# A hand-ordered schedule rewritten: attention fused with a gated feed-forward layer on one Trainium2 core

## The chip, the core and the metric

The kernel runs on one core of one Trainium2 chip. The core has four engines that compute: TensorE (PE in the profile; PEld is its weight load), VectorE (DVE), ScalarE (ACT) and GpSimd (POOL). SyncE (SP) only issues transfers. Each engine works off its own list of instructions strictly in order, so an instruction that waits holds up everything behind it on that engine. Transfers run on 16 DMA engines that all queues share. The metric is the time of one execution in microseconds. The kernel before takes 406.1 us, the median of three runs (405.54 to 406.79).

## The reference

The input is q, k and v, each 8 batches x 12 heads x 448 positions x 64 channels in fp32, a scalar tau of 0.1, and two weight matrices. The output is 3584 x 768 in fp32.

```python
q_n = q / (norm(q, axis=-1, keepdims=True) + 1e-06)
k_n = k / (norm(k, axis=-1, keepdims=True) + 1e-06)
attn = softmax(q_n @ k_n.transpose(0, 1, 3, 2) / tau)
x = (attn @ v).transpose(0, 2, 1, 3).reshape(8 * 448, 768)
h = x @ w_in                      # 768 -> 2048
out = (h * clip(h + 3, 0, 6) / 6) @ w_out   # 2048 -> 768
```

## The kernel before, in words

**Pairs.** Two heads are worked on together as a pair: 6 pairs to a batch, 48 in all, numbered through. Pairs 0 to 5 are the first batch, 6 to 11 the second. The two heads lie in the two halves of 128 partitions.

**Two regimes.** Pairs 18 to 47 run in a loop. Everything for pairs 0 to 17, about the first 120 us, is written out by hand in the list `PLAN`: strings of short operations that are issued in exactly that order. No scheduler moves anything (`tc.manual_schedule()`); the compiler only adds the waits that the data need. Each operation lands at the end of the list of its own engine, so the order in `PLAN` matters only within an engine. `ORDER` says which kind of product a unit `U` is.

**Operations.** A letter a, v or p picks ScalarE, VectorE or GpSimd. Items j are q or k of two pairs at once: items 0 and 1 are the queries and keys of pairs 0 and 1, items 2 and 3 those of pairs 2 and 3, and so on.

- `LQ.j`, `LV.d`: SyncE issues the load of item j (one transfer of 448 KB) or of the values of two pairs (four of 128 KB). Seven buffers hold the items: `LQ.j` waits for `NM.(j-7)`. Only eight of SyncE's transfers can be open at a time, because each waits for the eighth before it.
- `SQ.j` squares an item (for items 0 and 1 in pieces: `SQ.1.a.7.4` is four of the fourteen columns of 64). `RE.j` (DVE) adds the squares up; `NO.d` turns the sums of items 2d and 2d+1 into reciprocal norms: four small ScalarE instructions (ln, exp, ln, exp; lines 255 to 262), or with `v` two on ScalarE and then an add and a reciprocal on VectorE. `NM.j` multiplies the item by them into bf16.
- `TR.j`: seven TensorE transposes of an item into a PSUM bank (`Y`, `Z`, or the next of a ring). `CK`, `CQ`, `CS` copy keys and queries of one pair out of it to SBUF. From item 14 on the transposes are transfers (`XD`).
- `SC.i.g`, `EX.i.g`, `VA.i.g`: scores of pair i, group g of 4 (TensorE), exponential (ScalarE), product with the values (TensorE). `VC.i` casts the values to bf16 for it. `FI.i` (DVE) divides by the sum; `BK.i` and `CX.i` transpose the output on TensorE and copy it to `xT`, or `XP`/`XB` do it by transfer.
- Scores of pairs 0 to 5 go to two double-width PSUM tiles `SC`, so one exponential covers 128x896; `OPEN` then gives that PSUM to a ring of six banks, and from pair 6 on an exponential covers 128x448.
- `W`: the next of eight weight transfers, issued by GpSimd (line 910). The first four are `w_in`, the first two of them its left half; the last four are `w_out`.
- `U`: one unit of the feed-forward layer. The first 30 are `mm1_unit`: six matmuls of 128x448 with `w_in` (line 567). `UA` is its relu on ScalarE (line 576), `UV` the gated product on VectorE (line 582). The first unit needs `CX.0` to `CX.5` and both of the first two `W`. The last six are products with `w_out` (line 614) and need all eight `W`.
- `DP.n`: n matmuls on zeros, 128x248 (line 922), and `D.n`: 128x512 (line 917). Nothing reads what they write.
- `WS` and `GL` make sums of weights and copies for the loop (DVE).

The weights are taken like this, and a unit of the left half asks for two of them:

```python
    def next_weights():
        o, w = weights.pop(0)
        nc.gpsimd.dma_start(out=o, in_=w)
...
    def mm1_unit(b, fc):
        needs(*(("CX", i) for i in range(b * HP, (b + 1) * HP)))
        assert len(weights) <= 6 - 2 * (2 * fc // FCN)
```

Of the kernel before, what the change touches and what calls it, by code (L numbers as in the profile page):

```python
# [1097 lines left out]
```

## Time and profile before

| what | us |
|---|---|
| three runs, median (lowest to highest) | 406.1 (405.54 to 406.79) |
| the profiled execution, whole | 404.91 |
| its span, first to last instruction | 403.1 |
| PE, DVE, ACT, POOL busy | 395.5, 286.4, 278.3, 234.0 |

The profile shows one execution. Its span of 403.1 us and 1.8 us around it make its own 404.91 us, which is 1.2 us under the median of the runs. Busy times of matmuls overlap, since they are pipelined, and their ends are modelled: a busy TensorE is read from how closely the starts follow each other. A row of the timeline gives start and length in us, engine, line, operation, output<-input with their shapes and how many were merged; in square brackets stands the idle time before it and what ended it. Lines are those of the kernel before.

### The profile page before, as it was taken

What the parts mean: (1) busy time and instruction counts of PE and PEld (TensorE: products, weight loads), DVE (VectorE), ACT (ScalarE), POOL (GpSimd) and SP (SyncE); (2) the same over time, 40 slices, a digit from 0 to 9 for tenths busy, and PEclk for the clock granted to TensorE, in tenths of its full rate; (3) what the DMA queues carried; (4) which work ended last, traced back from release to release, by engine and by line L of the source; (5) the groups of instructions that cost most, each with busy time, mean ns of one, the idle gap of its engine ahead of it and who ended that gap; (6) DMA issues with size and microseconds to landing.
All of it is one profiled execution on the core that took longest, in us unless ns stands there. A gap on an engine that the chain in (4) does not pass through costs nothing.

```text
span 403.1 us, 9619 instructions
## 1 busy us (share of the span) xinstructions
PE 395.5 (98%) x3696; PEld 234.3 (58%) x3696; DVE 286.4 (71%) x503; ACT 278.3 (69%) x609; POOL 234.0 (58%) x228
## 2 busy tenths in 40 slices
PE   7999999999999999999999999999999999999996
PEld 4666656555655556556555556555565556555563
DVE  5898768766998777776867888687656566644663
ACT  5999998798467686786858768668658755225230
POOL 7799655662384997488386865766665500510070
PEclk9999999999999999999999999999999999999999
DMA  8999989979988659786989659976963523130134
GB/s 289 281 254 257 216 247 230 156 125 230 187 213 220 139 128 228 171 222 130 180 216 212 152 130 164 182 192 145 192 154 76 112 46 67 41 79 21 26 73 99
DMA packets 91566, 65.32 MB, mean 162 GB/s; under 512 B 56064, under 2 KB 89984, under 8 KB 91520
## 3 DMA queue, kind: packets, MB, share of 16 engines
q1 hardware_dynamic: 87408, 58.02, 62.8%
q0 software_dynamic: 3712, 6.29, 9.0%
q8 instruction: 29, 0.48, 0.5%
q10 hardware_dynamic: 400, 0.39, 0.3%
q14 instruction: 17, 0.14, 0.1%
HBM read 47.19 MB, written 11.01 MB: 144 GB/s over the span
## 4 chain that ended last, share of the span: by engine, by line
PE 94%; DVE 3%; DMA 1%; ACT 0%; issue 0%; DVEq 0%; ACTq 0%
PE M L567 24%; PE M L740 17%; PE PV L462 13%; PE Y L567 6%; PE M L422 6%; PE Z L567 5%; PE Y L740 4%; PE Z L740 4%; PE M L614 3%; PE M L820 2%; PE Z L422 2%; PE PV L922 2%; PE Z L820 1%; PE Y L422 1%; DVE n L238 1%; PE SC L422 1%
## 5 line engine op out<-in xcount | busy, mean ns | idle before, releaser
L440 ACT ACTIVATE at<-M 128x448 bf16<-128x448 f32 x200 | 99.9, 568 | 16.4 <-PE M L422 14.4
L567 PE MATMUL M<-xT,w_in_sb 128*128 128x448 bf16 x522 | 110.8, 352 | 0.0
L567 PEld LDWEIGHTS <-w_in_sb 128*128 128x128 bf16 x768 | 72.0, 98 | 62.6 <-issue 2.8
L274 POOL TENSOR_TENSOR nrm<-big,r 128x896 bf16<-128x896 f32 (+1 forms) x48 | 79.5, 1662 | 26.1 <-ACT r L262 19.3
L576 ACT ACTIVATE u<-M,bias 128x448 bf16<-128x448 f32 x87 | 57.0, 655 | 25.2 <-PE M L567 24.8
L582 DVE SCALAR_TENSOR_TENSOR gT<-u,M 128x448 bf16<-128x448 bf16 x76 | 46.7, 618 | 36.8 <-ACT u L576 36.3
L226 POOL TENSOR_TENSOR big<-big 128x896 f32<-128x896 f32 (+3 forms) x39 | 63.9, 1641 | 10.9 <-DMA big<-in_k_dram 5.7
L462 PEld LDWEIGHTS <-at 128*128 128x128 bf16 (+1 forms) x1536 | 54.9, 97 | 22.8 <-issue 13.5
L462 PE MATMUL PV<-vx,at 128*128 128x65 bf16 (+1 forms) x1536 | 64.3, 194 | 0.2 <-DVE on L483 0.2
L238 DVE TENSOR_REDUCE n<-big 128x14 f32<-128x896 f32 (+1 forms) x50 | 51.7, 1041 | 5.6 <-ACT big L224 4.6
L379 POOL COPY km<-tT 64x128 bf16<-64x128 bf16 x34 | 12.8, 376 | 58.1 <-DMA tT<-nrm 45.1
L769 POOL TENSOR_TENSOR big<-big 128x384 f32<-128x384 f32 x11 | 11.8, 1076 | 54.6 <-ACT big L788 54.5
L740 PEld LDWEIGHTS <-gT 128*128 128x128 bf16 x288 | 27.8, 98 | 20.0 <-DVE gT L718 0.6
L740 PE MATMUL M<-w_out_sb,gT 128*128 128x384 bf16 x208 | 37.9, 326 | 0.1
L440 ACT ACTIVATE at<-Z 128x448 bf16<-128x448 f32 x49 | 27.7, 565 | 9.9 <-PE M L422 7.3
L483 DVE TENSOR_TENSOR on<-PV,rc 128x512 bf16<-128x512 f32 x48 | 33.2, 691 | 1.7
L293 POOL CAST vx<-big 128x512 bf16<-128x512 f32 x44 | 33.2, 757 | 1.2 <-DMA big<-in_v_dram 1.1
L422 PE MATMUL M<-tT,kz 64*128 64x448 bf16 (+1 forms) x175 | 31.6, 351 | 0.0
L740 PEld LDWEIGHTS <-gs 128*128 128x128 bf16 x224 | 21.5, 98 | 14.8 <-DVE gs L718 0.4
L567 PE MATMUL Y<-xT,w_in_sb 128*128 128x448 bf16 x132 | 28.6, 352 | 0.0
L440 ACT ACTIVATE at<-Y 128x448 bf16<-128x448 f32 x45 | 25.7, 570 | 3.1 <-PE Z L422 1.7
L740 PE MATMUL M<-w_sum,gs 128*128 128x384 bf16 x144 | 26.3, 326 | 0.0
(130 smaller groups left out, 561.7 us busy)
## 6 DMA issues: line engine op xcount, KB each, us to landing
big<-in_v_dram SPq DMA_DIRECT2D x96, 128.0 KB, 4.4
big<-in_k_dram SPq DMA_DIRECT2D x24, 448.0 KB, 4.9
big<-in_q_dram SPq DMA_DIRECT2D x24, 448.0 KB, 4.4
out_dram<-o SPq DMA_DIRECT2D x107, 96.0 KB, 2.2
w_in_sb<-in_moe_w_in_dram POOLq DMA_DIRECT2D x4, 768.0 KB, 10.2
w_out_sb<-in_moe_w_out_dram POOLq DMA_DIRECT2D x4, 768.0 KB, 9.2
tT<-nrm SPq DMA_TRANSPOSE x34, 3.3
xT<-on SPq DMA_TRANSPOSE x25, 3.8
```

Of the source, the lines that this page charges most:

```text
L226: engines[e].tensor_tensor(out=o, in0=i, in1=i, op=ALU.mult)
L238: nc.vector.tensor_reduce(out=n2s[d % 2][:, j % 2, c], in_=sq[:, :, :, :].rearrange("p g c d -> p (g c) d")[:, c, :], axis=AX.X, op=ALU.add,)
L274: engines[e].tensor_tensor(out=nrm[:, :, g, :].rearrange("p c g d -> p g c d"), in0=raw_of[j][:, g, :, :], in1=rs[d % 2][3][:, j % 2, :] . ...
L293: (engines[e].copy if e == "a" else engines[e].tensor_copy)(out=o, in_=f)
L422: nc.tensor.matmul(o, ks, qt[rows], start=True, stop=True)
L440: nc.scalar.activation(out=o, in_=x, func=AF.Exp, scale=inv_tau)
L462: nc.tensor.matmul(pv_out(j, h), at[rows, n, q_cols(i // HP, j)], vt[rows, 3 + h if name == "M" else 5 * h + int(name[1]), :], start=(name ...
L483: nc.vector.tensor_tensor(out=on[:, :, :, :].rearrange("p j h d -> p h j d"), in0=pv4[:, :, :, 0:D], in1=rc[:, :, :].to_broadcast([128, 2, ...
L567: nc.tensor.matmul(ps[:, 0:S], w_in_sb[:, cc, fc * 128 : (fc + 1) * 128], x[:, cc, 0:S], start=(cc == 0), stop=(cc == CC - 1),)
L576: nc.scalar.activation(out=u[:, :], in_=ps[:, 0:S], func=AF.Relu, bias=half_bias, scale=1.0 / 6.0)
L582: nc.vector.scalar_tensor_tensor(out=g[:, fc, c0 : c0 + S], in0=u[:, :], scalar=1.0, in1=ps[:, 0:S], op0=ALU.min, op1=ALU.mult,)
L740: nc.tensor.matmul(m, lhs[:, c, :], rhs[:, c, c0 : c0 + width], start=(base is None and c == 0), stop=(c == KC - 1), skip_group_check=True,)
```

## The change

Only `PLAN` changes (the file has one line less, so every later line number is one lower). Both plans hold the same transfers and the same real TensorE work; the units `U`, and the parts of each pair, are issued in another order and some operations move to another engine. Of the dummies, 86 `DP` and 10 `D` become 69 `DP`: 58 of them ahead of the first scores and 11 behind, where before 37 `DP` and the 10 `D` stand ahead and 49 behind.

- `NO.0.0` and `NO.1` to `NO.6` take the form with two instructions on VectorE.
- To ScalarE: `SQ.4`, `SQ.11`, `SQ.21`, `CQ.10`, `CQ.12`. The pieces of items 0 and 1 are dealt out anew: GpSimd keeps one of item 0, VectorE has two of item 1, ScalarE the other four. From ScalarE to GpSimd: `SQ.6`, `SQ.13`, `SQ.15`, `SQ.18`, `SQ.20`. From ScalarE to VectorE: `CX.9`, `CK.12`.
- From VectorE to GpSimd: `NM.2`, `NM.18`, `VC.3`, `SQ.22`. From GpSimd to VectorE: `VC.4`, `VC.9`, `VC.15`, `VC.18`, `VC.19`.
- Products with the values come earlier: `VA.0.0` ahead of `SC.0.3`, `BK.0` ahead of `SC.2.0`. `CK.2` and `CK.3` stand behind `FI.0` and `CX.0`, `CK.6` and `CK.7` behind the copies of pair 2's output.
- On GpSimd the second `W` stands behind `SQ.6` to `SQ.9`, `NM.2` to `NM.7`, `VC.3` and `VC.5`; before, behind `SQ.4`, `SQ.7` to `SQ.9` and `NM.3` to `NM.6`. The third stands behind `SQ.10`, `SQ.13`, `SQ.12`. The fifth to eighth stand behind `SQ.17`, `VC.14`, `SQ.19` and `SQ.18`.
- On SyncE `LQ.7` goes ahead of `LV.1`, `LV.2` ahead of `LQ.9` to `LQ.11`, `LV.4` behind `LQ.13` and `LQ.12`.

Of the 35 and 34 lines the first half is shown; the rest follows the lists above.

```diff
--- before.py
+++ after.py
@@ PLAN @@
-    "LQ.1 DP.5 SQ.1.a.11.3 SQ.1.p.4.3 DP.1 SQ.1.a.0.4 LQ.0 SQ.0.p.8.6 DP.2 DP.4 LQ.3 LQ.2 SQ.1.v.7.4 RE.1.1",
-    "SQ.0.a.0.6 RE.1.0 NO.0.1 LQ.5 LQ.4 SQ.0.v.6.2 DP.6 NM.1.p.0 D.10 RE.0.1 DP.3 NM.1.p.1 RE.0.0 DP.8 NO.0.0",
-    "SQ.3.a.0.7 LV.0 DP.2 SQ.2.a.0.7 NM.0.p.0 RE.3 RE.2 NM.0.p.1 TR.1.Y DP.2 TR.0.Z CK.0.v DP.4 SQ.4.p.0.7 CQ.0.v",
-    "SQ.5.a.0.7 LQ.6 NO.1 LV.1 LQ.7 SC.0.0.0 SC.0.1.1 DP.5 DP.3 CQ.1.v EX.0.0 RE.5 RE.4 NM.3.p SC.0.2.0 CK.1.v DP.3",
-    "EX.0.1 DP.3 EX.0.2 NM.2.v DP.3 SC.0.3.1 TR.3.Y LQ.8 NO.2 EX.0.3 DP.3 SC.1.0.0 TR.2.Z EX.1.0 VC.0.v SC.1.1.1 DP.2",
-    "EX.1.1 VA.0.0 CK.2.v VC.1.v VC.3.v NM.4.p NM.5.p VA.0.1 LQ.9 SC.1.2.0 SQ.6.a.0.7 LQ.11 DP.5 DP.2 SC.1.3.1 EX.1.2",
-    "CQ.2.v LQ.10 LV.2 VA.0.2 VA.0.3 DP.3 SC.2.0.0 DP.2 EX.1.3 CK.3.v SC.2.1.1 EX.2.0 TR.4.Y SC.2.2.0 SQ.7.p.0.7",
-    "EX.2.1 RE.6 FI.0 RE.7 LV.3 VA.1.0 SQ.8.p.0.7 SC.2.3.1 CQ.3.v VC.2.v CQ.5.v VA.1.1 EX.2.2 SC.3.0.0 EX.2.3 VA.1.2",
-    "NO.3 RE.8 SC.3.1.1 CQ.4.v EX.3.0 DP.2 DP.4 EX.3.1 VA.1.3 TR.5.Z SC.3.2.0 W SQ.9.p.0.7 EX.3.2 FI.1 CK.4.v BK.0.Y",
-    "VA.2.0 SC.3.3.1 RE.9 LV.4 EX.3.3 NO.4 VA.2.1 VA.2.2 VA.2.3 SC.4.0.0 EX.4.0 NM.6.p DP.2 SC.4.1.1 SQ.10.p.0.7 W",
-    "SQ.11.p.0.7 EX.4.1 CX.0.v TR.6.Y CK.5.v FI.2 CQ.7.v VA.3.0 BK.2.Z RE.10 SC.4.2.0 EX.4.2 NM.7.p CQ.6.v VA.3.1",
-    "SC.4.3.1 DP.2 EX.4.3 CX.2.v SC.5.0.0 RE.11 VA.3.2 EX.5.0 SC.5.1.1 VA.3.3 VC.4.p SC.5.2.0 FI.3 VC.5.p EX.5.1",
-    "BK.1.Y TR.7.Z SC.5.3.1 CX.1.v CK.6.v CK.7.v VA.4.0 EX.5.2 DP.2 CS.7.v EX.5.3 BK.3.Y VA.4.1 LQ.12 CS.6.v OPEN",
-    "DP.2 CX.3.v NO.5 SC.6.0 VA.4.2 VA.4.3 SC.6.1 SC.6.2 EX.6.0 NM.8.p FI.4 EX.6.1 EX.6.2 SC.6.3 TR.8 BK.4 VA.5.0",
-    "CX.4.v VA.5.1 CQ.8.v SC.7.0 VA.5.2 EX.6.3 NM.9.p CQ.9.v VC.6.p VA.5.3 SC.7.1 FI.5 EX.7.0 SC.7.2 TR.9 SC.7.3",
-    "NM.10.p CK.8.v VA.6.0 EX.7.1 EX.7.2 VC.8.p CS.8.v W BK.5 SQ.12.p.0.7 LQ.13 VA.6.1 VA.6.2 SC.8.0 EX.7.3 CS.9.v",
-    "VA.6.3 CK.9.v DP.1 EX.8.0 CX.5.v SC.8.1 SC.8.2 VC.7.p FI.6 LQ.15 EX.8.1 U UA SQ.13.a.0.7 LV.5 U TR.10 EX.8.2 UA",
...
+    "DP.13 LQ.1 SQ.1.v.0.4 SQ.1.v.11.3 DP.9 DP.5 DP.3 SQ.1.a.7.4 LQ.0 SQ.0.p.8.6 SQ.1.a.4.3 SQ.0.a.0.6 DP.7 RE.1.0",
+    "RE.1.1 SQ.0.a.6.2 DP.5 LQ.2 LQ.3 NO.0.1 NM.1.p.0 NM.1.p.1 TR.1.Y RE.0.1 RE.0.0 NO.0.0.v LQ.5 DP.6 SQ.2.a.0.7",
+    "SQ.3.a.0.7 DP.4 RE.2 NM.0.p.0 RE.3 CK.1.v LQ.4 CK.0.v DP.3 NM.0.p.1 TR.0.Z SQ.4.a.0.7 LV.0 CQ.0.v DP.3 NO.1.v",
+    "SC.0.0.0 RE.4 NM.2.p LQ.6 SQ.5.a.0.7 SC.0.1.1 DP.4 VC.0.v DP.2 DP.2 EX.0.0 SC.0.2.0 EX.0.1 NM.3.p RE.5 VA.0.0",
+    "EX.0.2 SC.0.3.1 TR.2.Y CQ.1.v CQ.2.v CQ.3.v EX.0.3 SC.1.0.0 VA.0.1 LQ.7 VA.0.2 SC.1.1.1 VA.0.3 SQ.6.p.0.7 NO.2.v",
+    "SQ.7.p.0.7 EX.1.0 EX.1.1 SC.1.2.0 NM.4.p TR.3.Y VC.1.v LV.1 FI.0 CK.2.v EX.1.2 SC.1.3.1 BK.0.Z SC.2.0.0 VA.1.0",
+    "CX.0.v VC.2.v LQ.8 EX.1.3 LV.2 EX.2.0 CK.3.v SC.2.1.1 RE.6 VA.1.1 VA.1.2 SC.2.2.0 LQ.10 VA.1.3 EX.2.1 SC.2.3.1",
+    "TR.4.Y EX.2.2 FI.1 SC.3.0.0 EX.2.3 VA.2.0 NM.5.p VC.4.v SC.3.1.1 LQ.9 SQ.8.p.0.7 CQ.5.v EX.3.0 TR.5.Z EX.3.1",
+    "SC.3.2.0 VA.2.1 CQ.4.v VA.2.2 VC.3.p RE.7 CK.4.v DP.1 VA.2.3 BK.1.Y W FI.2 SC.3.3.1 EX.3.2 SC.4.0.0 NO.3.v",
+    "EX.3.3 SC.4.1.1 RE.8 SQ.9.p.0.7 CK.5.v VA.3.0 EX.4.0 EX.4.1 RE.9 SC.4.2.0 LQ.11 EX.4.2 VA.3.1 SC.4.3.1 VA.3.2",
+    "CX.1.v VA.3.3 EX.4.3 FI.3 NM.6.p NM.7.p BK.2.Z SC.5.0.0 SC.5.1.1 TR.6.Y NO.4.v LV.3 VA.4.0 EX.5.0 EX.5.1 VC.5.p",
+    "CQ.7.v CX.2.v SC.5.2.0 TR.7.Z EX.5.2 W VA.4.1 CQ.6.v VA.4.2 SQ.11.a.0.7 NM.8.p VC.7.p SC.5.3.1 CS.6.v VC.6.p",
+    "BK.3.Y CK.6.v CK.7.v EX.5.3 OPEN CS.7.v SC.6.0 VA.4.3 CX.3.v DP.2 EX.6.0 SC.6.1 EX.6.1 FI.4 SC.6.2 SC.6.3 NM.9.p",
+    "TR.8 EX.6.2 VA.5.0 SQ.10.p.0.7 BK.4 VA.5.1 VA.5.2 RE.11 EX.6.3 SC.7.0 EX.7.0 CX.4.v VA.5.3 CQ.9.v CQ.8.v SC.7.1",
+    "SC.7.2 TR.9 FI.5 EX.7.1 SC.7.3 LQ.13 CK.9.v VA.6.0 CS.8.v VA.6.1 EX.7.2 CK.8.v SQ.13.p.0.7 CS.9.v BK.5 VA.6.2",
+    "SC.8.0 VA.6.3 SC.8.1 EX.7.3 CX.5.v RE.10 FI.6 EX.8.0 SC.8.2 U RE.13 EX.8.1 U SC.8.3 EX.8.2 VA.7.0 SC.9.0 VA.7.1",
+    "NO.5.v LQ.12 SQ.12.p.0.7 VA.7.2 UA UV LV.4 U W VA.7.3 LQ.15 UA UV EX.8.3 EX.9.0 UA NM.11.p SC.9.1 RE.12 SC.9.2",
+    "UV U FI.7 NM.10.p TR.11 EX.9.1 NO.6.v LQ.14 VC.9.v EX.9.2 UA CS.10.v W TR.10 VC.8.p LV.5 SC.9.3 CK.10.v",
+    "SQ.15.p.0.7 CQ.11.a U VA.8.0 CQ.10.a VA.8.1 XP.6 EX.9.3 VA.8.2 CS.11.v LQ.17 NM.12.p UV CK.11.v VA.8.3 FI.8 UA",
...
```

## The prediction, made before the result was known

> **What bounds the kernel now.** I read the page's busy shares first, then its chain of waits, then busy time by stretch, then single engines' timelines about the joints between stretches.
>
> ```profile
> PE 395.5 (98%) x3696; PEld 234.3 (58%) x3696; DVE 286.4 (71%) x503; ACT 278.3 (69%) x609; POOL 234.0 (58%) x228
> PE 94%; DVE 3%; DMA 1%; ACT 0%; issue 0%; DVEq 0%; ACTq 0%
> ```
>
> TensorE holds 94% of the chain. Part of that is dummies, so I look at stretches (columns: span, then PE, PEld, DVE, ACT, POOL busy, granted clock, DMA share, GB/s). I cut at the first exponential (12.87), at the end of the last one of pair 5 (35.16), at the first unit U (42.85) and near the end of the plan (118).
>
> ```profile
> 12.87:35.16 22.29, 21.85 (x286) 14.25 (x285) 19.79 (x39) 21.22 (x39) 20.96 (x16) 1.00 1.06 267
> 35.16:42.85 7.69, 7.69 (x138) 5.21 (x134) 5.95 (x22) 7.53 (x21) 7.68 (x8) 1.00 1.11 247
> 42.85:118.00 75.15, 75.15 (x750) 43.88 (x749) 57.27 (x98) 60.52 (x135) 40.22 (x38) 1.00 0.98 200
> ```
>
> In the first row everything is full: ScalarE, TensorE with its 49 dummies, GpSimd, and the DMA engines. From 42.85 on TensorE never idles. Next, ScalarE in the first stretch:
>
> ```profile
> 12.87 2.54 ACT L440 ACTIVATE at<-SC 128x896 bf16<-128x896 f32 x3
> 15.28 0.24 ACT L255 ACTIVATE ln<-n 128x28 f32<-128x28 f32 x1
> ...
> 16.34 2.17 ACT L440 ACTIVATE at<-SC 128x448 bf16<-128x448 f32 x3
> 18.40 0.95 ACT L224 ACTIVATE big<-big 128x896 f32<-128x896 f32 x1
> ...
> 28.99 6.17 ACT L440 ACTIVATE at<-SC 128x896 bf16<-128x896 f32 x8
> ```
>
> Exponentials follow each other with only norms and one square between, so this row of work sets when pair 5 ends. Last, the joint at the first unit, and the weight transfer that it needs:
>
> ```profile
> 28.86 0.70 POOL L910 DMA_DIRECT2D w_in_sb<-in_moe_w_in_dram x1
> ```
> ```profile
> 42.54 0.35 PE L422 MATMUL M<-tT,kz 64*128 64x448 bf16 x2
> 42.85 0.35 PE L567 MATMUL M<-xT,w_in_sb 128*128 128x448 bf16 x1
> ```
> ```profile
> w_in_sb<-in_moe_w_in_dram POOLq DMA_DIRECT2D x1, 768.0 KB, 13.7
> ```
>
> The second W is issued at 28.86 and lands 13.7 us later (transfers issued in a window of its own), at 42.56: 0.3 us before the unit starts. TensorE came to it without idling, so today the weights are just in time. A plan that brings TensorE there earlier meets this transfer.
>
> The set of real TensorE operations ahead of the first U is the same in both plans, and so is the set behind it. With no idle time after 42.85, the end moves by what the first U moves, plus any new idle time behind it. I work on that.
>
> **The change part by part.** *ScalarE before the first exponential.* Gained: SQ.4, whose load, the sixth, is issued at 3.29 and lands 7.4 us later, at 10.70 (0.95 us, done 11.65). Lost: two of four norm instructions, half of the 1.06 us (15.28 to 16.34) that a norm takes. Then ln and exp of NO.1 to 12.15, SQ.5 to 13.0: first exponential at about 13.0, against 12.87. The first scores are ready by 12.5 (GpSimd's four half-size NM end near 11.0, transposes 0.55, copies 0.7).
>
> *ScalarE from there to the end of pair 5.* Kept: per pair three wide exponentials at 0.81 a step and one narrow at 0.45, six pairs: 17.3. Before, three norms at 1.06 and SQ.6 at 0.85 made 21.3, and waits and joints 1.0: the 22.29. After: three half norms at 0.5, SQ.11 in place of SQ.6, 0.85: 19.65. Walking the TensorE, VectorE and GpSimd lists beside it with row durations (reduce 1.0, copy 0.3, divide 0.85, GpSimd 896-wide 1.65, cast 0.57) I find waits of 0.2 for SC.3.0 and 0.2 at pair 5, so 20.0. Pair 5 ends at 33.0 instead of 35.16.
>
> *Norms on VectorE.* Seven times an add and a reciprocal on 28 columns. Not in the trace; nearest are the one-column memset, 0.06, and the 8-column reciprocal, 0.21: between 0.1 and 0.6 for the two, I take 0.35. It lies beside exponentials, but what is queued behind (RE.4, RE.8, CQ.7) moves by as much; that is in the walk.
>
> *Dummies.* 38 fewer behind the first scores, at 0.106 each (8.79, 1.54 for 13 with overlap): 4.0 us less on TensorE in a stretch where it was 21.85 of 22.29 busy. That is what lets TensorE follow the faster exponentials. Worth nothing by itself.
>
> *From the end of pair 5 to the first U.* Same work: 42.85 less 36.12, the first exponential of pair 6, is 6.73; before, a norm stood ahead of it (35.03 to 36.12) and now NO.5 is later. First exponential of pair 6 at 33.4, so TensorE is ready for the first U at 40.1: 2.7 us earlier.
>
> *The second W.* GpSimd can start NM.2 at 12.6 (NO.1 on VectorE). Up to the second W stand NM.2 to NM.7 and SQ.6 to SQ.9, ten at 1.65, two casts at 0.57 and the first W at 0.8: 18.4. Issue at 31.05, 2.2 us later than before; none of the ten waits for a load or norm in my walk. How long it takes is not settled by one row: the eight weight transfers took 7.3, 7.6, 9.8, 10.0, 10.4, 10.9, 13.7 and 14.4. The two longest were issued while another weight transfer was still open; the two shortest in quieter stretches. Here the loads of SyncE are the usual crowd (LQ.13, LQ.12, LV.4, LQ.15), but the first W, issued at 24.7, runs nearly alone because LQ.13 waits for NM.6 until 28.8. I take the median, 10.2: landing at 41.25, first U at 41.3. Ends: 7.3 (40.1, TensorE binds) and 13.7 (44.75).
>
> *SyncE.* LQ.7 now stands ahead of LV.1 and waits for NM.0 (11.0); LV.1 and LQ.8 queue behind. Four value transfers take 2.0 us (LV.1 lands from 14.6 to 16.2 before), so LV.1 lands near 17.5, for a first use at 19.1: free, and the DMA engines still have LQ.6 in hand until 14.2. LQ.13 waits for NM.6 (28.8) with LQ.12 and LV.4 behind it; these are used after 36, and the pause is what empties the queues for the first W.
>
> *Third and fourth W.* The third stands behind SQ.12, which waits for RE.10 (40.4): issue 42.1 instead of 40.00. The fourth stands behind NM.11 and NM.10: 46.3 instead of 42.89. The ninth U, at 60.3, is the first to need them. 46.3 and 10.2 is 56.5, free; with 14.4 it would cost 0.4.
>
> *Behind the first U.* TensorE has 19.0 us from the first to the ninth U; ScalarE in it 22 exponentials at 0.43, 8 relus at 0.62, three copies and two half norms: 16.9; VectorE 15. SC.10.0 to SC.10.2 follow copies CK.10, CK.11 and the fifth UV with under 0.1 us to spare, so I put 0.2 there; ends 0 and 1.0. Further on, XP.6 no longer holds SyncE's later loads as long (it waited to 51.28 for FI.7). The eighth W leaves at about 81 instead of 85.73, for a first use near 94.5 (95.89 before): covered, and if that cover went, a W of 14.4 us would cost 1. GpSimd gets five net squares and multiplies of 1.65 but sheds four casts; it idles 4 to 8 us at a time there.
>
> *Sum.* 41.3 less 42.85 is -1.55; plus 0.2: -1.35. The profiled 404.91 becomes 403.55. The runs' median lies 1.2 higher: 404.7.
>
> [...] The first 18 dummies take 3.90 us, 0.207 apart, the 13 at 8.79 run at 0.106: TensorE starts at half speed. [...]
>
> **The rivals.** (a) *W in time.* If the second W takes 7.3 to 9.8, the first U is at 40.1 to 40.9: 403.4 to 404.3. For: the first W runs alone. Against: five of eight rows are longer. (b) *W late, slower than before.* One mechanism: the second W takes as long as before or longer. At 13.7 the first U is at 44.8, 406.1 + 1.95 + 0.2 = 408.2; it decides against the change from 11.8 on (42.85). For: same neighbours on the DMA engines, full at 1.06 to 1.11. Against: it no longer queues behind an open W. [...] (d) *Scores don't get faster.* GpSimd's NM.6 and NM.7, or VectorE's copies, hold pair 5 until 35: TensorE meets W at about 42.85, 406.1. For: NM.7 ends at 30.5 in my walk and SC.5.3 follows at once. Against: it has 0.4 to spare.
>
> **How the numbers follow.** The likeliest, 0.40: W at 10 to 10.9, first U 41.1 to 42.0, 404.5 to 405.5; 404.7 is the point. By its own 0.3% line (1.2 us, about what a measurement of this kernel can tell from no change) it is 0.25 faster and 0.15 the same. (a) 0.18, faster. (d) with W between 11 and 12: 0.14, the same or slightly slower: 0.12 and 0.02. (b) 0.20, slower. (c) 0.08, slower. Faster 0.43, same 0.27, slower 0.30. The range leaves out (c) and the far end of (a): 403.4 to 408.2.
>
> **What would show it.** Right: the first exponential of pair 6 near 33.4; the second W issued near 31; TensorE idle about 1 us ahead of its first L567, ended by that transfer; that first L567 between 41 and 42; no idle TensorE after it. Wrong: no idle time there (W early, or scores late), granted clock under 1.00 after 40, or TensorE idle between the first and ninth unit, ended by VectorE's copies.

## The result and the profile after

The changed kernel takes **408.3 us** (median of 10 runs, 407.39 to 410.35) against 405.96 for the kernel before (10 runs, 405.13 to 407.14): ratio 1.0063, interval 1.0042 to 1.0084. It is slower by 0.6%, where I forecast 404.7 and a gain. (The ratios leave out single runs that lie more than 1.5% above a kernel's fastest; the medians and ranges in this text hold all runs.) The profiled execution took 408.33 us, span 406.5, mean granted clock 0.996; line numbers are one lower than before.

The page's busy shares and chain of the changed kernel:

```profile
PE 394.1 (97%) x3669; PEld 234.1 (58%) x3669; DVE 292.4 (72%) x518; ACT 274.1 (67%) x594; POOL 239.3 (59%) x228
PE 85%; DMA 6%; DVE 4%; ACT 1%; SPq 1%; issue 1%; POOL 1%; DVEq 0%; POOLq 0%; ACTq 0%
```

TensorE holds 85% of the chain instead of 94%: transfers have come into it (6% instead of 1%), VectorE a little (4% instead of 3%). Busy time by stretch, cut at the first exponential, at the end of the last one of pair 5, at the first unit and where the plan's last part ends (columns as in the prediction):

```profile
13.13:35.49 22.36, 19.12 (x262) 12.51 (x260) 20.10 (x47) 19.68 (x32) 21.04 (x16) 0.92 1.02 262
35.49:43.39 7.90, 7.05 (x116) 4.79 (x116) 6.92 (x19) 7.47 (x18) 5.93 (x6) 1.00 1.10 269
43.39:122.87 79.48, 77.72 (x756) 44.88 (x756) 62.03 (x106) 59.46 (x134) 51.30 (x43) 1.00 0.97 191
```

Pair 5 ends at 35.49, hardly elsewhere than before (35.16), although ScalarE was busy for only 19.68 of the 22.36 us: it waited. The granted clock is 0.92 in this row. And TensorE, which never idled behind the first unit before, does so for 1.76 us in the third row. What TensorE waited for between 13 and 122 us, by the view of waits (total, times, longest):

```profile
PE Z L495 <- DVE on L482: 1.4, 1, 1.4
PE M L566 <- DMA w_in_sb<-in_moe_w_in_dram: 0.8, 1, 0.8
PE SC L421 <- ACT at L439: 0.7, 2, 0.3
PE M L421 <- ACT at L439: 0.6, 1, 0.6
PE M L421 <- DVE gT L581: 0.6, 1, 0.6
PE Z L421 <- DVE kz L340: 0.5, 1, 0.5
PE M L421 <- POOL km L378: 0.4, 1, 0.4
PE Y L421 <- DVE o L626: 0.3, 1, 0.3
```

The span grew by 3.4 us. The first unit stands at 43.39 instead of 42.85: 0.55. The rest, 2.85, is lost behind it, at three places, where I compare the distance from one matrix product to the next with its usual one: 1.6 us at 53.2 to 55.1 (0.60, 0.94 and 0.26 over the usual, less the 0.19 that one such step always has), 0.5 at 105 and 0.6 at 112. These are the last four lines.

The second line is the second W. It leaves GpSimd at 32.76 (the row below) instead of 28.86 and lands 10.5 us later, at 43.26; the first unit follows 0.13 behind.

```profile
32.76 0.70 POOL L909 DMA_DIRECT2D w_in_sb<-in_moe_w_in_dram  x1
```

The longest wait, the first line, begins with one small instruction. VectorE's timeline of the changed kernel:

```profile
15.80 0.69 DVE L340 COPY tT<-Y 128x448 bf16<-128x448 bf16 x2
16.49 1.57 DVE L257 TENSOR_SCALAR le<-nr 128x28 f32<-128x28 f32 x1
18.16 0.33 DVE L258 RECIPROCAL r<-le 128x28 f32<-128x28 f32 x1
18.40 0.63 DVE L290 TENSOR_REDUCE vx<-big 128x512 bf16<-128x512 f32 x1
18.95 0.19 DVE L481 RECIPROCAL rc<-PV 128x8 f32<-128x8 f32 x1
19.17 0.69 DVE L482 TENSOR_TENSOR on<-PV,rc 128x512 bf16<-128x512 f32 x1
```

GpSimd and TensorE in the same stretch, a timeline each:

```profile
16.34 3.32 POOL L225 TENSOR_TENSOR big<-big 128x896 f32<-128x896 f32 x2
```

```profile
18.17 0.38 PE L418 MATMUL SC<-tT,kz 64*64 64x448 bf16 x2
19.92 0.40 PE L495 MATMUL Z<-ident,on 128*128 128x128 bf16 x4 [1.37 <-DVE on L482]
```

The add of EPS on 28 columns (norm NO.2, line 257) takes 1.57 us. Of the other six such adds one takes 1.88 (below) and five take 0.17 to 0.31. That of NO.2 starts behind the first of two GpSimd squares of 1.66 us and ends at 18.05, 0.03 after that square (16.34 to 18.02). What is queued behind it on VectorE, the reduce of values and pair 0's division, comes 1.4 us late; the first transposed output, BK.0, waits for the division; and TensorE, with BK.0 at the head of its list, is idle from 18.55 to 19.92. The scores behind BK.0 are late, so ScalarE waits 1.35 us at 19.3. Then the clock (busy time by stretch, same columns):

```profile
18.60:19.90 1.30, 0.00 (x0) 0.00 (x0) 1.27 (x4) 0.71 (x2) 1.30 (x2) 1.00 1.10 237
19.90:21.30 1.40, 1.38 (x20) 0.83 (x21) 1.21 (x4) 0.65 (x1) 1.40 (x2) 1.00 1.08 277
21.30:24.70 3.40, 3.40 (x37) 2.15 (x35) 2.76 (x7) 2.54 (x4) 3.40 (x4) 0.51 1.03 340
```

For 3.4 us, from 21.3 on, TensorE runs at half clock, and ScalarE waits three times more (0.31, 0.15 and 0.78). Together with the 1.35 that is 2.6 us, where my walk had 0.4.

### The profile page after: what moved, and what is told of

It is laid out like the page before. It is cut to its first block, busy times and chain, and to the rows that moved or that the text cites. A ratio compares the mean times of both kernels' runs of the same rounds, so it can differ in the third digit from the quotient of the medians.

```text
span 406.5 us, 9576 instructions
## 1 busy us (share of the span) xinstructions
PE 394.1 (97%) x3669; PEld 234.1 (58%) x3669; DVE 292.4 (72%) x518; ACT 274.1 (67%) x594; POOL 239.3 (59%) x228
## 4 chain that ended last, share of the span: by engine, by line
PE 85%; DMA 6%; DVE 4%; ACT 1%; SPq 1%; issue 1%; POOL 1%; DVEq 0%; POOLq 0%; ACTq 0%
PE M L566 24%; PE M L739 17%; PE PV L461 11%; PE Y L566 6%; PE Z L566 5%; PE M L421 5%; PE Y L739 4%; PE Z L739 4%; DMA big<-in_v_dram 3%; DMA w_in_sb<-in_moe_w_in_dram 3%; PE M L819 2%; PE Y L421 1%; PE Z L819 1%; PE M L613 1%; PE Z L421 1%
## 5 line engine op out<-in xcount | busy, mean ns | idle before, releaser
L439 ACT ACTIVATE at<-M 128x448 bf16<-128x448 f32 x195 | 97.0, 566 | 19.7 <-PE M L421 17.8
L273 POOL TENSOR_TENSOR nrm<-big,r 128x896 bf16<-128x896 f32 (+1 forms) x50 | 83.9, 1686 | 14.5 <-ACT r L261 8.3
L581 DVE SCALAR_TENSOR_TENSOR gT<-u,M 128x448 bf16<-128x448 bf16 x76 | 46.7, 618 | 40.6 <-ACT u L575 40.1
L225 POOL TENSOR_TENSOR big<-big 128x896 f32<-128x896 f32 (+2 forms) x41 | 70.1, 1711 | 9.1 <-DVE n L237 4.6
L292 POOL CAST vx<-big 128x512 bf16<-128x512 f32 x40 | 28.2, 707 | 14.3 <-DMA big<-in_v_dram 14.2
L439 ACT ACTIVATE at<-Y 128x448 bf16<-128x448 f32 x49 | 27.7, 565 | 3.2 <-PE Z L421 2.9
```

Source lines behind the costliest of these rows:

```text
L225: engines[e].tensor_tensor(out=o, in0=i, in1=i, op=ALU.mult)
L273: engines[e].tensor_tensor(out=nrm[:, :, g, :].rearrange("p c g d -> p g c d"), in0=raw_of[j][:, g, :, :], in1=rs[d % 2][3][:, j % 2, :] . ...
L292: (engines[e].copy if e == "a" else engines[e].tensor_copy)(out=o, in_=f)
L439: nc.scalar.activation(out=o, in_=x, func=AF.Exp, scale=inv_tau)
L581: nc.vector.scalar_tensor_tensor(out=g[:, fc, c0 : c0 + S], in0=u[:, :], scalar=1.0, in1=ps[:, 0:S], op0=ALU.min, op1=ALU.mult,)
```

## The experiments

Five links were to be told apart: the add, the sixth load (its square, SQ.4, now stands ahead of the first exponential on ScalarE), the clock, the second W, and the joints behind the first unit. Each kernel was timed beside the kernel before on the same chip. Edits are to the changed kernel's plan unless another is named. The last column is the run that was traced; where it lies far from its median, the trace tells of that run and not of the median.

| run | median us (all runs) | ratio to before (interval) | traced run |
|---|---|---|---|
| e13_again (changed kernel) | 408.21 (406.10 to 411.54) | 1.0061 (1.0035 to 1.0088) | 409.68 |
| e1_no_add | 407.78 (404.71 to 410.97) | 1.0022 (0.9998 to 1.0045) | 410.97 |
| e2_norms_back | 408.21 (405.84 to 412.25) | 1.0040 (1.0013 to 1.0067) | 409.65 |
| e3_dummies | 412.01 (408.72 to 413.91) | 1.0124 (1.0086 to 1.0161) | 413.00 |
| e5_w2_early | 408.62 (405.46 to 411.73) | 1.0043 (1.0018 to 1.0069) | 409.60 |
| e6_sq4_behind | 408.76 (408.11 to 412.15) | 1.0081 (1.0049 to 1.0114) | 408.54 |
| e7_before_sq4 | 407.93 (407.08 to 412.23) | 1.0054 (1.0027 to 1.0081) | 407.08 |
| e8_joint | 406.91 (405.74 to 408.41) | 1.0020 (1.0005 to 1.0035) | 406.65 |
| e9_all | 406.51 (404.38 to 408.10) | 1.0001 (0.9978 to 1.0024) | 407.66 |
| e10_front | 406.09 (405.20 to 409.90) | 1.0009 (0.9985 to 1.0033) | 406.29 |
| e11_dummies9 | 405.29 (404.31 to 408.26) | 0.9986 (0.9962 to 1.0010) | 408.26 |
| e12_late_w2 | 407.42 (405.46 to 410.54) | 1.0038 (1.0010 to 1.0066) | 405.60 |
| e14_adds_back | 406.87 (405.39 to 408.42) | 1.0019 (1.0000 to 1.0037) | 406.80 |
| e15_cs | 405.76 (404.81 to 407.80) | 1.0003 (0.9988 to 1.0018) | 406.13 |
| e16_dummies18 | 408.74 (406.81 to 410.33) | 1.0073 (1.0046 to 1.0099) | 409.55 |
| e17_mix | 405.15 (403.87 to 406.43) | 0.9979 (0.9960 to 0.9997) | 406.39 |
| e18_noadd_dummies | 408.49 (405.01 to 413.75) | 1.0038 (1.0010 to 1.0067) | 408.47 |
| e19_load_behind | 404.87 (404.08 to 406.46) | 0.9983 (0.9967 to 1.0000) | 406.32 |

The kernel before had medians of 405.6 to 406.3 beside them. Only the intervals of e9, e10, e11, e15, e17 and e19 lie wholly below both of the changed kernel's (1.0042 to 1.0084 and 1.0035 to 1.0088); those of e8 and e14 touch the second. Of the others e3 stands apart, slower; the rest differ from it by no more than the runs can tell, and what they show is read from the traces.

### The add

```diff
-            nc.vector.tensor_scalar(out=le, in0=nr, scalar1=EPS, scalar2=None, op0=ALU.add)
-            nc.vector.reciprocal(out=r, in_=le)
+            nc.vector.reciprocal(out=r, in_=nr)
```

> The changed kernel with the add of EPS left out of the seven norms that stand on VectorE (the reciprocal then reads the norm itself; EPS is missing from those divisors). Theory A: the 28-column add waits until GpSimd's running instruction ends (1.57 us at 16.49, 1.88 us at 50.37, against 0.17 to 0.31 for the other five), and that wait makes the 1.37 us of idle TensorE at 18.55, the half clock from 21.3 to 24.7, and the 1.1 us of idle TensorE at 53.3 to 54.8. Then: no half clock before 40 us, no idle TensorE near 53, second W issued about 0.8 earlier (near 32), first unit near 42.5 instead of 43.39, time 405.3 to 406.3; if a wait of TensorE for W of about 2 us then lowers the clock in its turn, up to 407.5. Theory B: the add only stands where VectorE waits for something else, and the second W sets the first unit: the wait moves to the reciprocal, the first unit stays at 43.4, 407.8 to 408.5.

```diff
-NO.2.v ... NO.6.v
+NO.2 ... NO.6
```

> The changed kernel with two of the seven norms, those of pairs 4 and 5 (NO.2) and of pairs 12 and 13 (NO.6), put back on ScalarE whole, as before; nothing left out. Theory A (the two long adds are the cause): as with the add left out, less about 0.5 us of ScalarE each: no half clock, no idle TensorE near 53, 405.5 to 406.7. Theory B (W sets the first unit, the adds are beside the path): 407.8 to 408.8.

Both missed theory A's times: 407.78 lies just above its upper end, 408.21 in theory B's range. Five of e1's twelve runs do lie at 404.7 to 406.4, as A says, the others at 407.5 to 411.0. Its trace is of the longest, 410.97. Without the add there is no idle time at 53 any more and BK.0 no longer waits, as A says. But in this trace the sixth load landed at 13.24 instead of 10.98, the first exponential stood at 15.40, TensorE idled for 1.94 us before 16.35, the clock was 0.50 up to 22, the second W, sent at 34.07, landed at 44.90, and the clock fell again at 114.35, with a wait of 1.93 that ended at 113.87. With two norms back on ScalarE the load came at 13.38, and another add, that of NO.3, now met a GpSimd instruction and took 1.04.

What the add does is told by all traces together. In eleven of them stand 69 such adds (the first of each trace on 14 columns). Of these 44 take 0.17 to 0.37 us. The other 25 take 0.55 to 2.08, and each of the 25 ends within 0.05 us of the end of a GpSimd instruction; no short one lies wholly inside a running compute instruction of GpSimd's (beside the issue of a weight transfer they take 0.30 to 0.37). Reciprocals of the same 28 columns take 0.33 beside GpSimd as without it. Why the add is held and the reciprocal is not, no run shows.

Later, in the version with the steady clock (e10, below), the adds were put back on VectorE:

```diff
-            nc.scalar.activation(out=le, in_=nr, func=AF.Identity, bias=eps_bias)
+            nc.vector.tensor_scalar(out=le, in0=nr, scalar1=EPS, scalar2=None, op0=ALU.add)
```

> The version with the rewritten front, with EPS added on VectorE again in all seven norms of the plan that stand there (as in the changed kernel) instead of on ScalarE; ScalarE sheds seven instructions of about 0.3 us, five of them ahead of the first unit. Theory A (an add waits for GpSimd's running instruction and what stands behind it on VectorE waits too): one to three of the adds take 0.6 to 1.9 us and end within 0.05 us of a GpSimd instruction, TensorE idles near 53 or ahead of the first outputs, 406.5 to 408 against 406.1 with the adds on ScalarE. Theory B (the adds cost nothing where the clock holds): ScalarE's relief shows, 404.8 to 405.8.

406.87 against 406.09, though ScalarE had less to do: theory A by the trace, less surely by the time, since the two ratios (1.0019 and 1.0009) have intervals that overlap. Three adds took 1.24, 0.62 and 0.88, TensorE waited 1.10 for BK.0, and the first unit moved from 42.66 to 43.40. The add of NO.6 was short this time, and there was no wait near 53.

That second place, in the changed kernel, VectorE's timeline and then GpSimd's:

```profile
50.37 1.88 DVE L257 TENSOR_SCALAR le<-nr 128x28 f32<-128x28 f32 x1
```

```profile
50.51 1.69 POOL L225 TENSOR_TENSOR big<-big 128x896 f32<-128x896 f32 x1
```

The add starts during a cast that runs to 50.57 and ends at 52.24, the square behind the cast at 52.20; the key copies behind it are late, and SC.10.0 and the scores next to it wait at 53.3 to 54.8: the 1.6 us.

### The sixth load

```diff
 (kernel before)
-SQ.4.p.0.7
+SQ.4.a.0.7
```

> The kernel before with one part of the change alone: SQ.4 on ScalarE instead of GpSimd, at its place ahead of SQ.5, NO.1 and the first exponential. Theory A: the first exponential follows the sixth load by 0.95 + 0.93 + 1.06 = about 2.9 us, so 13.7 for a load at 10.7 and 16.1 for one at 13.2, against 12.87; the first unit moves by about as much less 0.3: 406.8 to 408.7, and the runs spread more. Theory B (dummies and the wait for W cover it): 405.8 to 406.3.

407.93 against 406.26, and the interval lies clear of 1: theory A. The first exponential moved from 12.87 to 14.49 with the load at 10.60, 1 us more than worked out, because SQ.4 also waited for a reduce on VectorE; the first unit moved from 42.85 to 44.38.

```diff
-SQ.4.a.0.7 LV.0 CQ.0.v DP.3 NO.1.v SC.0.0.0 RE.4 ... SQ.5.a.0.7 ... EX.0.0 SC.0.2.0 EX.0.1 NM.3.p RE.5
+LV.0 CQ.0.v DP.3 NO.1.v SC.0.0.0 ... EX.0.0 SQ.4.a.0.7 SC.0.2.0 EX.0.1 NM.3.p RE.4 SQ.5.a.0.7 RE.5
```

> The changed kernel with the square of the sixth load (SQ.4) taken from ahead of the first exponential on ScalarE to behind it, the norm NO.1 first, SQ.5 and the reduce RE.4 one exponential later; same instructions. Theory A (the first exponential hangs on the sixth load: 2.15 us behind its landing in all five traces of the new order so far, at 10.98, 11.97, 13.21, 13.24 and 13.38): the first exponential stands at 12.7 to 13.0 whenever that load lands, the second W leaves 1 to 2 us earlier than in the other runs on this chip, and the time falls by 1 to 2 us: 406.5 to 407.5; the long adds and their clock loss stay. Theory B (the load's lateness is made up further on, as W and the joints decide): 408 to 408.7.

A miss: 408.76. The first exponential came at 12.41, but the copy that the second pair's scores need stood behind RE.5 on VectorE, which now waited for SQ.5; pair 1's first exponential came at 17.68 instead of 16.36. My edit moved the wait, it did not remove it.

The changed kernel itself again:

> The changed kernel itself again, on the chip of these runs, for a second trace of it. By all theories 408.0 to 408.8. The first exponential 2.15 us behind the sixth load's landing; an add on VectorE that ends with a GpSimd instruction near 17 to 19; at least one stretch of about 3.4 us at half clock behind idle TensorE.

408.21, with a trace (of a run of 409.68) in which the sixth load landed at 13.66. ScalarE's timeline of that trace:

```profile
13.74 0.95 ACT L223 ACTIVATE big<-big 128x896 f32<-128x896 f32 x1 [2.73 <-DMA big<-in_q_dram]
14.60 0.21 ACT L254 ACTIVATE ln<-n 128x28 f32<-128x28 f32 x1
14.84 0.23 ACT L255 ACTIVATE nr<-ln 128x28 f32<-128x28 f32 x1
14.97 0.93 ACT L223 ACTIVATE big<-big 128x896 f32<-128x896 f32 x1
15.81 0.90 ACT L439 ACTIVATE at<-SC 128x896 bf16<-128x896 f32 x1
```

SQ.4 waits 2.73 us for the load, and all that follows, the exponentials too, waits behind it. In the nine traces that have SQ.4 there the first exponential stands 2.15 or 2.16 us behind the landing, which is anywhere between 10.84 and 13.66. In the plan before ScalarE does not wait for this load, since GpSimd takes SQ.4.

The add of NO.2 took 1.57 here too, but TensorE, at half clock from 18.4 to 21.8, came to BK.0 as late as BK.0 was ready: it waited under 0.1 us for it, where it waited 1.37 in the first trace. Nor was there a wait behind the add of NO.6 (0.68). So which link costs the time differs from run to run of the same kernel.

### The clock

```diff
-SC.1.3.1 BK.0.Z
+SC.1.3.1 DP.12 BK.0.Z
```

> The changed kernel with 12 dummy matrix products (1.27 us) in TensorE's list ahead of the first transposed output (BK.0), where TensorE stood idle for 1.37 us at 18.55. Theory A with the clock as a link of its own: the add still takes about 1.5 us, ScalarE still waits 1.35 at 19.3, but the granted clock stays 1.00 to 25 us; the joints of ScalarE behind 21 (0.31, 0.15, 0.78) shrink, the second W leaves up to 0.8 earlier, first unit 42.5 to 42.8: 407.3 to 407.8, with a smaller spread of the runs. Theory B (the clock costs nothing at the end, as W decides): first unit 43.4, 408.0 to 408.6.

412.01, slower by 3.8 than the changed kernel. In this trace the idle time lay elsewhere: 2.57 us before 16.32, for the sixth load, which landed at 13.21, with a clock of 0.59 from 17.6 to 21.4. By the time TensorE reached the dummies (22.15) BK.0 was ready (22.10), so they were 1.27 us of delay. The second W left at 35.33 and took 12.1 us, TensorE idled for 2.59 before the first unit at 47.53, and the clock fell again (0.53 from 48.2 to 51.7).

```diff
-DP.4 VC.0.v DP.2 DP.2 EX.0.0 SC.0.2.0 EX.0.1 ... SC.0.3.1
+DP.4 VC.0.v DP.14 EX.0.0 SC.0.2.0 DP.4 EX.0.1 ... SC.0.3.1 DP.4
```

> The changed kernel with 18 more dummies between the scores of pair 0 (10 ahead of SC.0.2, 4 ahead of SC.0.3, 4 behind it): 1.9 us of dummies where TensorE idled for 0.3 to 2.2 us. Theory A (idle TensorE lowers the clock, and that is a link of its own): granted clock 1.00 up to the first output in most runs, the slowest runs (409 to 412) gone, median 407.2, which is where the ten runs of the changed kernel lead when their times are drawn against their mean clock to 1.000. Theory B (the clock's loss is covered or the dummies only take its place): 408.2 or more.

408.74: theory B's number. The idle time at the first scores was filled, but BK.0 still waited (1.49 us, behind an add of 1.62), and the clock fell behind it.

```diff
 (e1_no_add)
-DP.4 VC.0.v DP.2 DP.2 EX.0.0 SC.0.2.0 EX.0.1 ... SC.0.3.1
+DP.4 VC.0.v DP.14 EX.0.0 SC.0.2.0 DP.4 EX.0.1 ... SC.0.3.1 DP.4
```

> The changed kernel with EPS left out of the seven norms on VectorE (no add, as in e1_no_add) and the 18 dummies of e16_dummies18 between the scores of pair 0. Theory A (idle TensorE lowers the clock, and that costs by itself): without the add the only long idle time up to 30 us is that for the sixth load, and the dummies fill it: clock 1.00 up to the first unit, median 405.5 to 406.7 against 407.78 without the dummies, slowest run under 409. Theory B (the late sixth load costs the time, not the clock): 407.5 to 408.2, as wide a spread.

The time, 408.49, is no better than without the add alone (407.78); the trace is the most telling of all. Its busy time by stretch and TensorE's timeline at the first unit:

```profile
13.00:42.90 29.90, 26.30 (x394) 18.02 (x391) 26.63 (x63) 28.81 (x53) 28.28 (x21) 1.00 1.08 267
42.90:46.30 3.40, 3.18 (x9) 1.31 (x10) 0.62 (x3) 1.02 (x4) 3.26 (x4) 0.50 1.07 186
```

```profile
40.47 0.35 PE L421 MATMUL M<-tT,kz 64*128 64x448 bf16 x2
43.12 0.90 PE L566 MATMUL M<-xT,w_in_sb 128*128 128x448 bf16 x2 [2.30 <-ACT ln L254]
```

Here the prediction's walk comes nearest to true: the clock stays at 1.00, pair 6 has its first exponential at 34.11 (forecast 33.4), and TensorE is ready for the first unit at 40.82 (forecast 40.1), 2 us earlier than before. The second W, sent at 31.34, lands at 42.98, and the unit starts 0.14 after it, as in the changed kernel (0.13); the view names ScalarE's last instruction before the start, which the unit does not use. So TensorE stands still for 2.30 us, and near its end the clock falls, for 3.4 us. The granted clock is 0.94 in those 2.30 us and 0.50 behind them.

What speaks for the clock as a cost of its own, without showing it: in the ten runs of the changed kernel the time goes with the mean clock, 407.4 to 407.9 at 0.998 and 0.999, 410.0 at 0.990 (correlation -0.82; the line through them reaches 407.15 at 1.000). By that line the clock would cost about 1.2 of the 2.35 us, an estimate and an upper one, because the waits ahead of the falls also lengthen a run by themselves. No single edit showed it: each filled idle time reappeared elsewhere.

### The second W

```diff
-SQ.9.p.0.7 CK.5.v ... EX.5.2 W VA.4.1
+SQ.9.p.0.7 W CK.5.v ... EX.5.2 VA.4.1
```

> The changed kernel with the second W issued on GpSimd right behind SQ.9, ahead of NM.6, NM.7 and VC.5 (issue near 28.2 instead of 32.76); no other engine's order changes. Theory A: W lands between 38.4 and 42, TensorE's own arrival sets the first unit: near 42.6 instead of 43.39, no idle time ahead of it; the rest stays, 407.5. If TensorE's arrival is not what is left (W at 14 us or more again because the first W is still open): 43.4, 408.3.

W left at 29.21 and landed at 39.07, and no idle time stood before the first unit, which came at 45.02: TensorE's own arrival was late (first exponential 14.13, adds of 1.57, 1.43 and 0.92, half clock from 35). 408.62, no gain. Once the front was free (e10 below), the W's place did count:

```diff
 (e10_front)
-SQ.9.p.0.7 W CK.5.v ... EX.5.2 VA.4.1
+SQ.9.p.0.7 CK.5.v ... EX.5.2 W VA.4.1
```

> The same as the version with the rewritten front, but the second W at the changed kernel's place, behind NM.6, NM.7 and VC.5. If the second W sets the first unit once the front is free: issue near 32, landing 42 to 43.5, TensorE idle 1.5 to 2.5 us ahead of the first unit, 1.5 to 2 us slower than with the W early: 405.5 to 406.5, more if that idle time lowers the clock. If not: within 0.3 of it.

407.42 against 406.09, with intervals that overlap. The trace explains less than that: W left at 32.16 and landed at 43.09, TensorE idled for 0.56 and the unit moved from 42.66 to 43.23. But it is of a run of 405.60; those up to 410.54 have no trace.

### The joints behind the first unit

VectorE's timeline of the changed kernel at the last of them, and GpSimd's:

```profile
106.67 2.00 DVE L688 TENSOR_TENSOR w_sum<-w_out_sb 128x3072 bf16<-128x3072 bf16 x1
108.60 3.23 DVE L688 TENSOR_TENSOR w_out_sb<-w_out_sb 128x3072 bf16<-128x3072 bf16 x1
111.75 0.55 DVE L626 COPY o<-Y 128x384 f32<-128x384 f32 x1
```

```profile
107.02 3.19 POOL L225 TENSOR_TENSOR big<-big 128x896 f32<-128x896 f32 x1
110.18 3.20 POOL L273 TENSOR_TENSOR nrm<-big,r 128x896 bf16<-128x896 f32 x1
```

In these rows the two engines take turns. GpSimd's square (1.65 alone) waits until the first sum ends at 108.67, then runs to 110.21; the second sum (1.75 alone) waits for that and ends at 111.83; GpSimd's multiply waits for it again. The copy that frees an output bank stands behind, and a score waits for the bank.

```diff
-WS.1 VA.16.1 UA SC.17.0 WS.y3 EX.17.0 SC.17.1 LV.11 EX.17.1 UV WS.7.0
+WS.1 VA.16.1 UA UV SC.17.0 WS.y3 EX.17.0 SC.17.1 LV.11 EX.17.1 WS.7.0
```

> The changed kernel with the VectorE copy of one finished output block (a UV of the plan) ahead of the weight sum WS.y3 instead of behind it; nothing else. Theory A (the copy stands behind two weight sums that GpSimd's work stretches from 1.75 to over 3 us, and a score waits for its bank): the idle TensorE before the score near 112 to 114, 0.28 in the changed kernel's trace and 1.5 to 1.9 in the four on this chip, is gone: 406.4 to 407.7. Theory B (the score waits there for keys or the exponential all the same): no change, 408 to 408.7.

406.91, and the idle time is gone: theory A. Of the single edits this one and e1 have the lowest ratios. The wait at this place was 0.28 us in the changed kernel's first trace, 0.92 in its second and up to 1.93 in those of other edits (e1), so taking it away can gain more than the first trace tells.

```diff
 (e10_front)
-VC.16.p FI.14 EX.15.2 VC.17.p LV.10 ... CS.16.v WS.6
+FI.14 EX.15.2 LV.10 ... CS.16.v VC.16.p VC.17.p WS.6
```

> The version with the rewritten front, with two casts of value tiles (VC.16, VC.17) on GpSimd behind the key copies of pair 16 (CS.16) instead of ahead of them; nothing else. Theory A (the key copies are held by casts that wait for value loads): TensorE's 1.16 us of idle time at 104 is gone, 405 to 405.5 against 406.1. Theory B (the score there waits for something else at the same time): no change, 406.

The wait at 104 is gone: theory A for the place. The time, 405.76 against 406.09, lies between A's and B's and within the noise; 1.01 us of a new wait came up at 127.6, for a transposed output.

### All together

```diff
 (e6, e5 and e8 edits, and)
-            nc.vector.tensor_scalar(out=le, in0=nr, scalar1=EPS, scalar2=None, op0=ALU.add)
+            nc.scalar.activation(out=le, in_=nr, func=AF.Identity, bias=eps_bias)
```

> The changed kernel with all four causes taken away: SQ.4 behind the first exponential, the second W behind SQ.9, the output copy ahead of WS.y3, and EPS added on ScalarE (one 28-column instruction, about 0.22 us) so that VectorE's norms are a reciprocal alone. If these four are what cost the time: first exponential near 12.8, first unit at 40 to 41 with TensorE idle under 0.5 ahead of it, clock 1.00, no idle time behind it over 0.3: 403.4 to 404.8, faster than before. If the earlier first unit runs into something else (a weight transfer, VectorE's copies): 405 to 406.5, and the trace shows the wait.

Taken away together, the four links are what the change had lost: the ratio is 1.0001 (0.9978 to 1.0024) against 1.0061. The expected gain over the kernel before (403.4 to 404.8) did not come. The runs fall into two groups, six from 404.38 to 405.61 and six from 407.41 to 408.10. The trace is of the second: VA.0.0, now reached early, waited 1.92 us for the first value load, and the clock was 0.53 from 16.6 to 23.9.

```diff
 (e9_all)
-RE.5 VA.0.0
+RE.5 DP.12 VA.0.0
```

> The version with four causes taken away, with 12 dummies (1.27 us) ahead of VA.0.0, where its trace has TensorE idle for 1.92 us at 14.15, followed by half clock from 16.6 to 23.9; nothing else. Theory A (the idle time there makes the clock fall in half of the runs): runs at 404.3 to 405.8 only, median 405. Theory B (the clock falls for another reason, or dummies only fill what is then missing elsewhere): two groups as before, or all later by up to 1.3: median 406.5 to 408.

405.29, seven of twelve runs at 404.3 to 405.3, the others up to 408.26; the trace (408.26) has 0.98 and 1.08 us of idle time there all the same, and one fall. Between A and B, and not clear of e9's noise.

```diff
 (e9_all)
-... SC.0.1.1 DP.4 VC.0.v DP.2 DP.2 EX.0.0 SQ.4.a.0.7 SC.0.2.0 EX.0.1 NM.3.p RE.4 SQ.5.a.0.7 RE.5 VA.0.0 EX.0.2 SC.0.3.1 TR.2.Y CQ.1.v CQ.2.v CQ.3.v EX.0.3 SC.1.0.0 VA.0.1
+... SC.0.1.1 CQ.1.v DP.8 EX.0.0 SQ.4.a.0.7 SC.0.2.0 DP.6 EX.0.1 NM.3.p RE.4 SQ.5.a.0.7 VC.0.v TR.2.Y CQ.2.v CQ.3.v RE.5 SC.0.3.1 DP.6 EX.0.2 EX.0.3 VA.0.0 VA.0.1 SC.1.0.0
```

> The kernel with all four causes taken away, and the front once more rewritten: the copy CQ.1 ahead of the reduces of the fifth and sixth tile, the first values product (VA.0.0) and its copy behind the fourth exponential and RE.4 so that neither TensorE nor VectorE waits for the first value load, and 20 dummies instead of 8 between the first scores. If waits for loads and the clock loss that follows them are what is left (six of the twelve runs of the version with four causes away stand at 404.4 to 405.6, six at 407.4 to 408.1): granted clock 1.00 throughout, first unit 40.3 to 41.5, all runs between 403.3 and 405.5, median 404.2. If the clock has nothing to do with the two groups, they stay: median near 406.5.

Eleven of twelve runs lie within 405.20 to 406.82 and the clock is 1.00 in the trace: the spread went, as expected. The median did not come down to 404.2. The first unit is at 42.66, not 40.3 to 41.5: the squares SQ.4 and SQ.5 and the EPS instructions now stand among the exponentials on ScalarE, and TensorE idled 1.16 us at 104. So I relieved ScalarE of the EPS where VectorE was free to add it:

```diff
 (e15_cs)
+            if d in (2, 3, 6): nc.scalar.activation(out=le, in_=nr, func=AF.Identity, bias=eps_bias)
+            else: nc.vector.tensor_scalar(out=le, in0=nr, scalar1=EPS, scalar2=None, op0=ALU.add)
```

> The version of e15_cs, with EPS added on ScalarE only for the norms of pairs 4 to 7 and 12 and 13 (d = 2, 3 and 6), on VectorE for the other four, where GpSimd was idle or near the end of an instruction. If ScalarE up to the end of pair 5 is what sets the first unit in this version (0.6 us less there): first unit near 42.1, 404.6 to 405.2, faster than before by 0.2 to 0.3 per cent. If VectorE's adds get held after all: 405.5 to 406.5.

405.15, first unit at 42.08: as expected. Ratio 0.9979 (0.9960 to 0.9997). One more wait was left in its trace (view of waits); its stretch up to the first unit, by busy time, is without a fall of the clock:

```profile
PE M L567 <- DMA xT<-on: 1.6, 1, 1.6
```

```profile
12.41:42.08 29.67, 26.53 (x393) 18.32 (x392) 25.25 (x61) 28.53 (x51) 26.95 (x20) 1.00 1.05 258
```

```diff
 (e17_mix, behind the plan)
-    do("LQ", FIRST + 6)          ahead of pair 18
+    do("LQ", FIRST + 6)          behind the transposed output of pair 17
```

> The version of e17_mix with the key load of pair 24 and 25 on SyncE behind the transposed output of pair 17 instead of ahead of it (the load's issue took 2.1 us at 121.58 in that trace, the transposition left at 123.80 and landed at 127.44). If that issue holds the transposition: TensorE's idle time before the unit near 127 under 0.3, 404.0 to 404.7 against 405.15. If the transposition waits for its own input or a queue: no change, 405 to 405.4.

404.87, a little above the 404.0 to 404.7 expected, and the wait at 127 is gone. In this trace 1.93 us of another stand at 138.55, for a VectorE instruction; six runs are at 404.1 to 404.6. Between 122 and 398 TensorE idles for 2.1 us here and 1.9 in e17, against 0.2 in the kernel before: more than the 0.8 that the first unit gains in these two traces, and no run settles why. Against the kernel before these two versions are 0.2% faster, at the edge of what the runs can tell.

## Why the prediction was wrong

**First exponential: right in this trace, wrong as a rule.** 13.13 against about 13.0. But I entered the sixth load at its landing in one trace, 10.70, with no other end, though the change was the first to put it on the path. It lands from 10.54 to 13.67 in the traces, and SQ.4 put there in the plan before costs 1.7 us (e7).

**Norms on VectorE: the step that failed.** "Between 0.1 and 0.6 for the two, I take 0.35" holds where GpSimd is idle (0.17 and 0.33). Twice in the changed kernel the add alone took 1.57 and 1.88, behind a GpSimd instruction. In the changed kernel's first trace BK.0's wait (1.37 us), with the fall of the clock behind it (0.51 for 3.4 us), and the 1.6 us at 53 follow from these two. My nearest rows, a memset and a reciprocal, were of the wrong kind: rows of a weight sum (1.74 alone) and a cast (0.57) that stretch beside each other stood in the trace of before, VectorE's and GpSimd's:

```profile
101.06 2.61 DVE L689 TENSOR_TENSOR w_sum<-w_out_sb 128x3072 bf16<-128x3072 bf16 x1
```

```profile
102.01 2.14 POOL L293 CAST vx<-big 128x512 bf16<-128x512 f32 x1
```

**Scores: "waits of 0.2 and 0.2" were 2.6.** The busy part was right: 19.68 us of ScalarE against 19.65 worked out. With the waits pair 5 ended at 35.49 and TensorE was ready for the first unit at 42.63, not 40.1. Rival (d), scores no faster, came true, but not by the engine's load that I named. With add and front idle time gone (e18) it was ready at 40.82.

**Dummies: "worth nothing by itself" left out the clock.** With 38 fewer, 1.37 us of idle time came with a fall for 3.4 us; in e16 and e18 the clock stayed at 1.00 as far as TensorE had dummies for its waits. But neither run was faster for it, so that their removal costs time is not shown.

**The second W: flight right, start wrong.** 10.5 us against 10.2; but it left at 32.76 instead of 31.05. GpSimd started NM.2 0.45 later, SQ.9 waited 0.5 for a reduce on VectorE (its load had landed at 24.67), NM.6 0.8 for NO.3, late from ScalarE's waits. First unit 43.39, not 41.3. TensorE did idle ahead of the unit for this transfer, 0.76 us, as forecast, but at 42.63 and not at 40.1. Rival (b)'s time, 408.2, was met by luck: not the flight of W was long, its start was late. The chance of 0.08 for (c), a clock that falls as TensorE waits for this W, was my estimate: the trace of before has no fall (1.00 in the three rows shown). In the changed kernel's first trace the clock stayed at 1.00 behind the 0.76 us; in e18 it fell to 0.50 behind 2.30.

**Behind the first unit: 0.2 was 2.85.** I had named SC.10 as tight, with an end of 1.0; the second add made it 1.6. The joints at 105 and 112 were not in my walk at all, although key copies, casts and weight sums had new neighbours there; it ended at the ninth unit.

**Sum.** 2.1 of the first unit and 2.65 behind it are 4.75, which is, but for rounding, what lies between 403.55 and 408.33. That the adds, SQ.4, the late W and the joint at 112 together make the loss is shown by e9. Single prices, by medians: the adds put back with a steady clock 0.8 (e14; 0.4 by the ratios, not clear of noise), SQ.4 put into the plan before 1.7 (e7), the late W put back with a free front 1.3 (e12, not clear of noise), the joint at 112 taken away 1.4 (e8). They don't add up, since each link hides the next. How the loss divides among them, and the clock's share, stays open.

## What to carry to other kernels

Price a small VectorE instruction by what GpSimd runs at that moment, not by its size, and look for its kind, not its shape, among the rows: the adds of 28 columns took 0.17 to 2.08 us, the reciprocals of the same columns 0.33. An order that moves an instruction behind a load makes that load's spread its own (the sixth load landed from 10.54 to 13.67): give the landing both ends. Where several links hide one another, undoing one shows little; take all away, then put one back.

## What the hardware showed that I had not expected

The granted clock fell to about half (0.50 to 0.53) behind idle times of 1.37 us (changed kernel), 2.30 (e18), 1.92 (e9) and 1.04 (e5, at 33.8 to 34.8), but not behind 1.37 at 19.5 in e5, nor behind 1.96 before the first unit in e6 (1.00 from 44.5 to 50), nor behind 1.95 in e13 and 1.93 in e19. The falls lasted 3.41 us, but for one of 6.83 each in e1 and e9. So the length of an idle time did not tell whether a fall followed; what does, these runs do not show.

An add of 28 columns took up to 2.08 us, 12 times its quickest, and a 1.75 us sum 3.23; the profile counts all of it as busy time.

The same load, sent at 3.3 us in every trace, landed between 10.54 and 13.67, with the same five loads ahead of it.
